# First decay rows of an attention and two-FFN kernel copied inside SBUF, its masks and loads issued in another order, and its first weight chunks loaded in pieces

## The chip, the cores and the metric

One core of a Trainium2 chip runs the whole program. The metric is the device time in microseconds (us) from launch to end; the median of the runs is quoted. The kernel is written with one program per engine: TensorE (PE, with its weight loads PEld), VectorE (DVE), ScalarE (ACT), GpSimd (POOL), and SyncE (SP), which here only issues DMA transfers.

## What is computed

The reference is a causal attention with a forgetting gate, and behind it two feed-forward layers:

```python
def _attn_ref(q, k, v, f):                 # (4, 8, 576, 64), f (4, 8, 576)
    scores = scale * np.matmul(q, k.transpose(0, 1, 3, 2))
    cum = np.cumsum(np.log(np.clip(f, 0.0001, 1.0)), axis=-1)
    decay = cum[:, :, :, None] - cum[:, :, None, :]
    scores = np.where(causal, -1000000000.0, scores + decay)
    attn = np.exp(scores - np.max(scores, axis=-1, keepdims=True))
    attn = attn / (np.sum(attn, axis=-1, keepdims=True) + 1e-09)
    return np.matmul(attn, v)
...
x = attn_out.transpose(0, 2, 1, 3).reshape(2304, 512)
h = x @ w_in;  x = (h - np.tanh(h)) @ w_out          # 512 -> 2048 -> 512
h = x @ w_in2; x = (h / (1 + np.exp(-h))) @ w_out2   # 512 -> 2048 -> 512
```

## The kernel before

**Attention.** The 32 heads are worked on as 16 pairs of heads. A pair has nine score tiles: four blocks of 128 query rows for each head, and one tile for the last 64 rows of both heads. A loop over `n` takes one tile in a step (line 734), 144 steps for 16 pairs and some to drain: PE makes the scores of tile n + 2, DVE takes the masked minimum of tile n (`least`, L497), ACT the exponential of tile n - 1 (L515), GpSimd divides three finished tiles by their row sums (`normalise`, L529), PE transposes tile n - 9 (L543), and two steps on it multiplies by the values (L588). All is in float32; each operand is split into a high and a low float32r part.

**Preparing a pair.** `load_kq` (L373) brings keys and queries of a pair (608 KB) into `kqraw`. `split` rounds them to `kqhi` (the keys on GpSimd, L393, the queries on DVE, L396) and makes `kqlo` as the rest on GpSimd (L384). `place` then copies both inside SBUF into the operand tiles `kqa` and `kqb` by DMA (L381): `place(p, 0)` six copies of `kqhi`, 608 KB for a head, 1216 KB in all; `place(p, 1)` four copies of `kqlo`, 608 KB; `place(p, 2)` reads four decay rows for each head from `dec` (L423). `kqraw` has two buffers, `kqhi` and `kqlo` one, the operand tiles two. Steps for pair p + 1 are hung on the loop by the table `prep`: the split from step 9p - 5 on, the places at 9p - 2 and 9p - 1, the load of pair p + 2 at 9p - 8.

**The decay rows.** `decay_rows` (L104) turns f into the cumulative log (a scan, L114) and four rows for each head that add the decay to the scores as a matmul. They are stored to DRAM as `dec` (L636) and read back. Pair 0 does without the operand tiles: its scores are four matmuls of 64 rows each (L459), the last of which takes the decay rows that `first_dec` (L412) reads from `dec` into `kqa0`; the tile of the last 64 query rows (L475) takes them from `last_q[2]`, a part of `ptl`.

**Order.** The order is that of the code (a manual schedule): each engine runs its instructions as they are written. SP issues all DMAs one after another. A DMA uses one of eight landing semaphores in turn, and waits for the landing of the one eight before it.

**The weights.** 32 chunks, each 512 KB of `w_in` and 512 KB of `w_out`, are loaded by `wload` (L135, DMA in L141) as 64-bit numbers and decoded in 14 stages (`wstages`, `wdecode`). For the first five chunks the stages `rest` (L177) and `join` (L181) run on GpSimd. Chunks 0 and 1 are loaded at steps 5 and 9 and their 28 stages done at steps 11 to 132, two in nine steps; each later chunk is loaded when the one two before it is decoded. Layers 1 and 2 (L256, L315) follow the attention.

Of the kernel before, what the change touches and what calls it, by code (L numbers as in the profile page):

```python
# [19 lines left out]
SCALE = 0.125  # L20
# [19 lines left out]
def forgetting_attention_two_ffn(  # L40
# [25 lines left out]
    def setup_mask(const):  # L66
# [8 lines left out]
        return mask, eps  # L75

    def setup_later(const):
        mask4 = const.tile([P, S // 2], F32, name="mask4")
        nc.gpsimd.memset(mask4, 0.0)
        for j in range(2):  # L80
            m = mask4[64 * j:64 * j + 64, S // 2 - 64:]
            nc.gpsimd.affine_select(
                out=m, in_=m, pattern=[[-1, 64]], compare_op=ALU.is_ge,
                fill=MASKED, base=0, channel_multiplier=1,
            )
        ident = const.tile([P, P], F32, name="ident")
# [5 lines left out]
        return mask4, ident  # L92
# [4 lines left out]
    C0, C1 = slice(S, S + 512), slice(S + 512, S + 576)  # L97

    def decay_consts(rows):
        nc.gpsimd.memset(rows[:, 0::2, S:RAW], 1.0 / SCALE)  # L100
        nc.gpsimd.memset(rows[:, 1::2, KQ], 1.0 / SCALE)
        nc.gpsimd.memset(rows[:, :, C1], 0.0)

    def decay_rows(rows, scratch, ft, meanwhile):  # L104
# [30 lines left out]
    def wload(k):  # L135
# [53 lines left out]
    def wdecode(k, left=0):  # L189
# [138 lines left out]
    def attention():  # L328
        with ExitStack() as actx:
# [56 lines left out]
            def split(p, j):  # L386
# [5 lines left out]
                if j == 0 and p:  # L392
# [226 lines left out]
            rows = room[:, 0:4 * RAW].rearrange("p (r w) -> p r w", w=RAW)  # L619
# [188 lines left out]
```

## Time and profile before

| what | value |
|---|---|
| median of 3 runs | 1026.9 us (1024.64 to 1027.33) |
| profiled execution, its own time | 1028.68 us |
| its span, first to last instruction | 1026.5 us |
| mean granted TensorE clock | 0.996 |
| PE busy | 990.1 us, 96% of the span |
| DVE, ACT, POOL busy | 59%, 48%, 19% |
| DMA moved | 83.71 MB |

The span is the profiled execution from its first to its last instruction; the device time has 2 us more around it. The page cuts the span into 40 slices of 25.7 us. Only in the first is PE busy less than eight tenths (3 of 10); from the second on it is at 7 and then 9. The DMA engines stand at 6 to 9 tenths in the first eight slices, which are the attention, and at 0 to 2 after it. A granted clock of 1.00 is 2.4 GHz, 0.50 is 1.2 GHz.

### The profile page before, as it was taken

What the parts mean: (1) busy time and instruction counts of PE and PEld (TensorE: products, weight loads), DVE (VectorE), ACT (ScalarE), POOL (GpSimd) and SP (SyncE); (2) the same over time, 40 slices, a digit from 0 to 9 for tenths busy, and PEclk for the clock granted to TensorE, in tenths of its full rate; (3) what the DMA queues carried; (4) which work ended last, traced back from release to release, by engine and by line L of the source; (5) the groups of instructions that cost most, each with busy time, mean ns of one, the idle gap of its engine ahead of it and who ended that gap; (6) DMA issues with size and microseconds to landing.
All of it is one profiled execution on the core that took longest, in us unless ns stands there. A gap on an engine that the chain in (4) does not pass through costs nothing.

```text
span 1026.5 us, 13933 instructions
## 1 busy us (share of the span) xinstructions
PE 990.1 (96%) x4928; PEld 828.3 (81%) x4928; DVE 608.5 (59%) x1382; ACT 492.5 (48%) x1092; POOL 200.2 (19%) x288
## 2 busy tenths in 40 slices
PE   3799999998999999999999999999999999999998
PEld 3577788777898888988888888888888888888887
DVE  4589888978686536666566774442552556633323
ACT  3588798885455333334343444343444344433222
POOL 5678987986000000000000000000000000000000
PEclk9999999999999999999999999999999999999999
DMA  6989999722211101110011220100110111001111
GB/s 158 289 233 236 265 234 243 198 94 84 82 59 66 42 1 42 61 64 29 14 41 42 83 82 0 42 28 35 62 30 12 42 42 42 1 1 42 41 42 62
DMA packets 28792, 83.71 MB, mean 82 GB/s; under 512 B 4340, under 2 KB 4340, under 8 KB 28692
## 3 DMA queue, kind: packets, MB, share of 16 engines
q1 hardware_dynamic: 28724, 82.83, 27.3%
q8 instruction: 39, 0.64, 0.3%
q14 instruction: 29, 0.24, 0.1%
HBM read 49.46 MB, written 5.34 MB: 53 GB/s over the span
## 4 chain that ended last, share of the span: by engine, by line
PE 88%; DVE 4%; DMA 4%; ACT 2%; SPq 2%; issue 1%; POOL 0%; DVEq 0%; ACTq 0%; POOLq 0%
PE a L315 38%; PE h L256 38%; PE out_t L588 4%; PE t L543 3%; SPq L381 1%; PE s L462 1%; PE s L463 1%; DMA kqb<-kqhi 1%; DMA kqa<-kqhi 1%; DVE kqhi L396 1%; PE s L479 1%; DVE ptl L570 1%; DMA kqraw<-kq 1%; PE misc L479 0%; ACT p L515 0%
## 5 line engine op out<-in xcount | busy, mean ns | idle before, releaser
L256 PE MATMUL h<-xh,wh 128*128 128x512 f32 (+1 forms) x640 | 237.2, 371 | 0.0
L256 PE MATMUL h<-xl,wh 128*128 128x512 f32 (+1 forms) x640 | 235.5, 368 | 0.0
L256 PE MATMUL h<-xh,wl 128*128 128x512 f32 (+1 forms) x640 | 235.5, 368 | 0.0
L278 DVE TENSOR_TENSOR gl<-g,gh 128x512 fp32r<-128x512 f32 (+1 forms) x158 | 101.4, 642 | 101.7 <-ACT gh L274 99.7
L274 ACT CAST gh<-g 128x512 fp32r<-128x512 f32 (+1 forms) x160 | 92.6, 579 | 95.9 <-DVE g L271 93.3
L256 PEld LDWEIGHTS h<-xh,wh 128*128 128x128 f32 x640 | 120.7, 189 | 21.1 <-issue 0.7
L256 PEld LDWEIGHTS h<-xl,wh 128*128 128x128 f32 x640 | 120.6, 188 | 21.0 <-issue 0.7
L256 PEld LDWEIGHTS h<-xh,wl 128*128 128x128 f32 x640 | 120.6, 188 | 20.1
L315 PE MATMUL a<-gh,wh 128*128 128x512 f32 (+1 forms) x320 | 117.9, 369 | 0.0
L315 PE MATMUL a<-gl,wh 128*128 128x512 f32 (+1 forms) x320 | 117.8, 368 | 0.0
L315 PE MATMUL a<-gh,wl 128*128 128x512 f32 (+1 forms) x320 | 117.7, 368 | 0.0
L315 PE MATMUL a<-wh,gh 128*128 128x512 f32 x288 | 112.2, 390 | 0.0
L315 PE MATMUL a<-wl,gh 128*128 128x512 f32 x288 | 112.2, 390 | 0.0
L315 PE MATMUL a<-wh,gl 128*128 128x512 f32 x288 | 112.0, 389 | 0.0
L273 ACT ACTIVATE g<-h 128x512 f32<-128x512 f32 (+1 forms) x80 | 44.3, 554 | 113.6 <-PE h L256 98.5
L244 DVE TENSOR_TENSOR xl<-y,xh 128x512 fp32r<-128x512 f32 (+1 forms) x60 | 37.4, 638 | 96.6 <-ACT xh L242 96.6
L242 ACT CAST xh<-y 128x512 fp32r<-128x512 f32 (+1 forms) x60 | 34.2, 579 | 104.8 <-PE h L256 103.1
L515 ACT ACTIVATE p<-p,mn 128x128 f32<-128x128 f32 (+3 forms) x128 | 72.2, 565 | 24.7 <-DVE mn L497 20.5
L529 POOL TENSOR_SCALAR p<-p,sm 128x128 f32<-128x128 f32 (+3 forms) x128 | 70.6, 565 | 19.4 <-DVE sm L526 14.8
L244 DVE TENSOR_TENSOR xl<-x,xh 128x512 fp32r<-128x512 f32 (+1 forms) x56 | 34.5, 634 | 62.3 <-ACT xh L242 62.3
L543 PE MATMUL t<-ident,p 128*128 128x128 f32 x320 | 59.6, 286 | 9.6 <-DVE sm L522 6.6
L315 PEld LDWEIGHTS a<-gh,wh 128*128 128x128 f32 x320 | 60.3, 189 | 10.4 <-ACT x L599 0.4
(136 smaller groups left out, 1705.2 us busy)
## 6 DMA issues: line engine op xcount, KB each, us to landing
raw<-w_in SPq DMA_DIRECT2D x32, 512.0 KB, 3.3
raw<-w_out SPq DMA_DIRECT2D x32, 512.0 KB
kqraw<-kq SPq DMA_DIRECT2D x16, 608.0 KB, 5.0
kqa<-kqhi SPq DMA_DIRECT2D x30, 304.0 KB, 4.7
vraw<-v SPq DMA_DIRECT2D x16, 320.0 KB, 5.3
kqa<-kqhi SPq DMA_DIRECT2D x30, 160.0 KB, 4.0
kqb<-kqlo SPq DMA_DIRECT2D x30, 160.0 KB, 3.1
out<-ob SPq DMA_DIRECT2D x18, 256.0 KB, 2.0
```

Source lines behind the costliest of these rows:

```text
L242: nc.scalar.copy(hi[:, :n], src[:, k, t0:t0 + n])
L244: eng.tensor_tensor(lo[:, :n], src[:, k, t0:t0 + n], rd(hi[:, :n]), ALU.subtract)
L256: nc.tensor.matmul(hp[:, :n], w[:, k * P:k * P + P], m[:, :n], start=(k == 0 and r == 0), stop=(k == NKT - 1 and r == 2),)
L273: nc.scalar.activation(g[:, :n], hp[:, :n], AF.Silu)
L274: nc.scalar.copy(gh[:, :n], g[:, :n])
L278: eng.tensor_tensor(gl[:, :n], g[:, :n], rd(gh[:, :n]), ALU.subtract)
L315: nc.tensor.matmul(dst, w, m, start=(first and r == 0), stop=(last and r == 2))
L381: nc.sync.dma_start(out=rd(out), in_=rd(in_))
L515: nc.scalar.activation(pt[:, :w], pt[:, :w], AF.Exp, bias=mn, scale=-1.0, accum_out=rowsum[n // 3][:, n % 3:n % 3 + 1],)
L529: nc.gpsimd.tensor_scalar(pt[:, :w], pt[:, :w], sm[:, j:j + 1], 1.0, ALU.mult, ALU.mult)
L543: nc.tensor.transpose(tp[:, c, :], pt[:, c * P:c * P + P], ident)
L588: nc.tensor.matmul(dst, w, pt[:, 448 * c + a:448 * c + q1], start=(c == 0 and r == 0), stop=(c == last and r == len(terms) - 1),)
```

## The change

- `first_dec` copies the decay rows of pair 0 from `rows` in SBUF to `kqa0`, one DMA for each of the four rows, two from SP's queue and two from ACT's. The tail parts for `last_q[2]` still come from `dec`, by `first_dec_last`, behind `place(1, 0)`.
- The rows in `rows` and `dec` are without the gap of 64 zeros (576 KB rather than 608 KB), so `place(p, 2)` is two DMAs, and the gap in `kqb` is set to zero once (GpSimd).
- Both masks, and the zeros of the operand tiles, are made on GpSimd ahead of the splits of pair 0; the identity stays late. Pair 1's first cast goes from GpSimd to DVE.
- `load_kq(2)` is issued ahead of `place(1, 1)`. The preparing of pair 2 comes two steps later, the loads of pair 3 four steps later.
- The loads of chunks 0 to 3 are cut into 4 pieces for each of the two matrices, 128 KB each. They go into a list, `trickle`, from which each step issues one. Chunk 0 starts at step 20, chunk 1 at step 36. The 28 stages lie on steps 40 to 132.

```diff
-        return mask, eps
-
-    def setup_later(const):
         mask4 = const.tile([P, S // 2], F32, name="mask4")
...
+        return mask, eps, mask4
+
+    def setup_ident(const):
...
-    C0, C1 = slice(S, S + 512), slice(S + 512, S + 576)
+    QS = slice(S, 2 * S)
...
-        nc.vector.tensor_copy(r(1, C0), cum[:, 0:512])
-        nc.vector.tensor_copy(r(1, TAIL), cum[:, 512:S])
-        nc.vector.tensor_tensor(r(3, C0), cum[:, 0:512], rows[:, 1, C0], ALU.subtract)
-        nc.vector.tensor_tensor(r(3, TAIL), cum[:, 512:S], rows[:, 1, TAIL], ALU.subtract)
+        split(0, 1)
+        nc.vector.tensor_copy(r(1, QS), cum)
+        nc.vector.tensor_tensor(r(3, QS), cum, rows[:, 1, QS], ALU.subtract)
...
-    def wload(k):
+    trickle = []
+
+    def wload(k, pieces=1):
...
+            to, n = r.rearrange("p n w -> p (n w)"), 2 * DM // pieces
+            for j in range(pieces):
+                trickle.append((to[:, n * j:n * j + n], (w_in, w_out)[m][l][c][:, n * j:n * j + n]))
             raws[k, m] = r
+        if pieces == 1:
+            begin(len(trickle))
+
+    def begin(n):
+        for to, source in trickle[:n]:
+            nc.sync.dma_start(out=to, in_=source)
+        del trickle[:n]
...
-                wload(k + 2)
+                wload(k + 2, 4 if k < 2 else 1)
...
-                if j == 0 and p:
+                if j == 0 and p > 1:
...
             def first_dec():
+                to = rd(first[2]).rearrange("(h r) w -> h r w", h=2)
+                for r in range(4):
+                    (nc.scalar if r % 2 else nc.sync).dma_start(
+                        out=to[:, r, 0:S + 512], in_=rows[0:2, r, 0:S + 512]
+                    )
+
+            def first_dec_last():
                 for h in range(2):
                     r = slice(64 * h, 64 * h + 4)
-                    nc.sync.dma_start(out=rd(first[2][r]), in_=dec[h])
-                    nc.sync.dma_start(out=rd(last_q[2][r, 64 * h:64 * h + 64]), in_=dec[h, :, TAIL])
+                    nc.sync.dma_start(out=rd(last_q[2][r, 64 * h:64 * h + 64]), in_=dec[h, :, S + 512:2 * S])
...
-                    nc.sync.dma_start(
-                        out=rd(tb[64:68, :, K0:W]), in_=dec[2 * p:2 * p + 2].rearrange("h r w -> r h w")
-                    )
+                    src = dec[2 * p:2 * p + 2].rearrange("h r w -> r h w")
+                    nc.sync.dma_start(out=rd(tb[64:68, :, K0:Z1]), in_=src[:, :, 0:S + 512])
+                    nc.sync.dma_start(out=rd(tb[64:68, :, Q1:W]), in_=src[:, :, S + 512:2 * S])
...
-            for h in range(2):
-                place(1, 0, [h])
-                place(1, 1, [h])
-                if h == 0:
-                    place(1, 2)
+            place(1, 0)
+            first_dec_last()
+            place(1, 2)
             load_kq(2)
+            place(1, 1)
             load_v(1)
...
-                                later(9 * p + k, fn, p + 1, j)
+                                later(9 * p + k + (2 if p == 1 else 0), fn, p + 1, j)
                         elif p + 2 < NP and (p or fn is load_v):
-                            later(9 * p + k, fn, p + 2)
+                            later(9 * p + k + (4 if p == 1 else 0), fn, p + 2)
...
-            ahead = {-N + 5: [(wload, 0)], -N + 9: [(wload, 1)], -12: [(open_earlier,)], 0: [(open_early,)]}
+            ahead = {-N + 20: [(wload, 0, 4)], -N + 36: [(wload, 1, 4)], -12: [(open_earlier,)], 0: [(open_early,)]}
...
-                at(9 * (k // 2 + 1) + (2, 6)[k % 2] - N, wdecode, k // NSTAGE, NSTAGE - 1 - k % NSTAGE)
+                at(40 + (N - 48) * k // (2 * NSTAGE) - N, wdecode, k // NSTAGE, NSTAGE - 1 - k % NSTAGE)
...
+                begin(1 if n < N else len(trickle))
```

How the instructions move. SP's queue at the start, before: after the store of `dec`, four reads of it for pair 0 and five copies for pair 1 come these rows (`kqraw2` is the load for pair 2, `raw0_0` weight chunk 0):

```order
L423 DMA kqb1_105<-dec_153 4x2x1216
L381 DMA kqa1_104<-kqhi1_163 64x1216
L381 DMA kqa1_104<-kqhi1_163 64x640
L381 DMA kqb1_105<-kqhi1_163 64x576
L381 DMA kqa1_104<-kqlo1_164 64x576
L381 DMA kqb1_105<-kqlo1_164 64x640
L373 DMA kqraw2_182<-kq 128x1216
L378 DMA vraw1_184<-v 128x640
L373 DMA kqraw3_232<-kq 128x1216
L141 DMA raw0_0_0_285<-w_in0 128x1024
L141 DMA raw0_0_1_287<-w_out0 128x1024
L423 DMA kqb0_103<-dec_153 4x2x1216
```

And now, from the decay rows of pair 0 (`kqa0<-x`) on:

```order
L424 DMA kqa0_102<-x_69 2x1088 x2
L657 DMA dec_168<-x_69 32x4608
L391 DMA kqa1_104<-kqhi1_170 64x1216
L391 DMA kqa1_104<-kqhi1_170 64x640
L391 DMA kqb1_105<-kqhi1_170 64x576
L391 DMA kqa1_104<-kqhi1_170 64x1216
L391 DMA kqa1_104<-kqhi1_170 64x640
L391 DMA kqb1_105<-kqhi1_170 64x576
L431 DMA ptl_111<-dec_168 4x64 x2
L440 DMA kqb1_105<-dec_168 4x2x1088
L441 DMA kqb1_105<-dec_168 4x2x64
L383 DMA kqraw2_188<-kq 128x1216
```

The load for pair 2 has moved ahead of the four copies of `kqlo1`, the two tail reads behind the six copies of `kqhi1`, and weight chunk 0 out of this stretch.

SP's queue where the pieces of chunk 0 now stand, between the load for pair 5 and the copies for pair 4:

```order
L383 DMA kqraw5_538<-kq 128x1216
L151 DMA raw0_0_0_563<-w_in0 128x256 x4
L151 DMA raw0_0_1_564<-w_out0 128x256
L440 DMA kqb0_103<-dec_168 4x2x1088
L441 DMA kqb0_103<-dec_168 4x2x64
L391 DMA kqa0_102<-kqhi4_602 64x1216
L391 DMA kqa0_102<-kqhi4_602 64x640
L391 DMA kqb0_103<-kqhi4_602 64x576
L391 DMA kqa0_102<-kqhi4_602 64x1216
L391 DMA kqa0_102<-kqhi4_602 64x640
L391 DMA kqb0_103<-kqhi4_602 64x576
L151 DMA raw0_0_1_564<-w_out0 128x256
```

Five pieces stand in a row ahead of `place(4, 2)` and `place(4, 0)`, one between `place(4, 0)` and `place(4, 1)`, and two behind it.

GpSimd's rows around the last stage of one matrix of chunk 0, before:

```order
L529 TENSOR_SCALAR p6_1_1_1416<-p6_1_1_1416,sm60_1436 128x256
L529 TENSOR_SCALAR p6_1_2_1441<-p6_1_2_1441,sm60_1436 128x384
L529 TENSOR_SCALAR p6_1_3_1471<-p6_1_3_1471,sm60_1436 128x512
L181 TENSOR_TENSOR wl0_0_0_764<-wl0_0_0_764,wb0_0_0_959 128x512
L393 TENSOR_SCALAR kqhi9_1573<-kqraw9_1320 128x576
```

The same stage now:

```order
L394 TENSOR_TENSOR kqlo10_1784<-kqraw10_1527,kqhi10_1783 128x320
L191 TENSOR_TENSOR wl0_0_0_1300<-wl0_0_0_1300,wb0_0_0_1435 128x512
L394 TENSOR_TENSOR vhl9_1913<-vraw9_1822,vhl9_1913 128x5x64
L545 TENSOR_SCALAR p8_1_1_1819<-p8_1_1_1819,sm78_1838 128x256
L545 TENSOR_SCALAR p8_1_2_1843<-p8_1_2_1843,sm78_1838 128x384
```

It has moved from a place directly ahead of a pair's `kqhi` to one behind its `kqlo`. Of the eight GpSimd stages of chunks 0 and 1, three stood directly ahead of a `kqhi` before and two do now.

## Rows read from the trace of the kernel before

**Rows 1.** Chain that ended last, in order of time: start us, us, what.

```profile
10.25 4.33 DMA dec<-x
...
24.49 5.13 DMA kqraw<-kq
...
128.61 3.05 DMA kqb<-kqlo
...
245.71 2.72 PE h L256 x12
```

**Rows 2.** By stretch: us; busy PE, PEld, DVE, ACT, POOL; clock; DMA share; GB/s.

```profile
14.60:27.58 12.98, 10.38 (x33) 8.38 (x33) 2.99 (x12) 3.49 (x10) 3.05 (x10) 1.00 0.77 169
...
45.25:59.59 14.34, 13.35 (x75) 10.83 (x74) 9.96 (x41) 9.83 (x31) 9.87 (x16) 0.88 0.94 251
59.59:71.29 11.70, 11.57 (x75) 9.56 (x74) 10.69 (x40) 10.40 (x33) 9.71 (x16) 1.00 0.90 238
...
107.13:120.51 13.38, 11.49 (x75) 9.54 (x74) 12.03 (x41) 10.46 (x34) 11.98 (x18) 1.00 0.91 250
120.51:133.85 13.34, 13.07 (x75) 10.91 (x74) 9.46 (x39) 10.14 (x30) 10.80 (x17) 0.87 0.97 265
```

**Rows 3.** Timeline of PE: start us, us, what, [idle before <- what ended it].

```profile
16.80 0.44 PE L459 MATMUL s<-kqa 64*128 64x128 f32 x1 [7.54 <-DMA kqa<-dec]
...
22.00 0.44 PE L475 MATMUL s<-kqa,ptl 128*128 128x288 f32 x1
...
31.13 0.79 PE L459 MATMUL s<-pth 64*128 64x512 f32 x1 [3.96 <-DVE mn L497]
...
33.14 0.47 PE L462 MATMUL s<-kqa 128*128 128x128 f32 x1
...
44.30 0.41 PE L543 MATMUL t<-ident,p 128*128 128x128 f32 x2 [3.20 <-DVE sm L522]
...
45.31 0.31 PE L462 MATMUL s<-kqa 128*128 128x128 f32 x1
```

**Rows 4.** Timeline of DVE at the start, same columns.

```profile
8.74 1.42 DVE L120 SCALAR_TENSOR_TENSOR x<-x 32x576 fp32r<-32x576 f32 x1
...
10.09 0.52 DVE L396 CAST kqhi<-kqraw 128x640 fp32r<-128x640 f32 x1
...
17.40 0.29 DVE L497 CUSTOM_DVE_ANT_0 p<-s,mask 128x128 f32<-128x128 f32 x1 [6.79 <-POOL mask L82]
...
29.84 0.49 DVE L396 CAST kqhi<-kqraw 128x640 fp32r<-128x640 f32 x1 [4.44 <-DMA kqraw<-kq]
...
43.06 0.49 DVE L396 CAST kqhi<-kqraw 128x640 fp32r<-128x640 f32 x1 [2.65 <-DMA kqb<-kqhi]
```

**Rows 5.** Timeline of SP's DMA queue: issue us, us of issuing, what.

```profile
15.98 1.16 SPq L381 DMA_DIRECT2D kqa<-kqhi  x2
...
26.49 0.43 SPq L141 DMA_DIRECT2D raw<-w_in  x1
...
30.89 2.81 SPq L381 DMA_DIRECT2D kqa<-kqhi  x2
...
56.22 0.58 SPq L373 DMA_DIRECT2D kqraw<-kq  x1
...
59.59 0.27 SPq L423 DMA_DIRECT2D kqb<-dec  x1
```

**Rows 6.** Weight loads by line (L141), from issue to landing.

```profile
DMA to landing us min/median/max: 3.2/3.3/4.0
```

**Rows 7.** Busy time in the two us from 46.00, columns as in rows 2.

```profile
46.00:48.00 2.00, 2.00 (x8) 1.62 (x8) 2.00 (x10) 0.91 (x4) 2.00 (x4) 0.50 1.04 394
```

**Rows 8.** DVE's casts of one line from 45 to 205 us: ns min/median/max.

```profile
L396 DVE CAST kqhi<-kqraw x12: 487/494/2833, 57.4 to 191.2; 128x640 fp32r<-128x640 f32 x12
```

**Rows 9.** Timeline around the longest of these casts, DVE and GpSimd.

```profile
115.98 2.83 DVE L396 CAST kqhi<-kqraw 128x640 fp32r<-128x640 f32 x1
...
116.56 1.27 POOL L181 TENSOR_TENSOR wl<-wl,wb 128x512 fp32r<-128x512 f32 x1
```

More of the change, by code (lines that the diff above doesn't have):

```diff
@@ L64, in rd, with setup_masks @@
         return ap.bitcast(F32)
-    def setup_mask(const):
+    def setup_masks(const):
         mask = const.tile([P, 640], F32, name="mask")
@@ L91, in setup_later, with decay_rows @@
         )
-        return mask4, ident
+        return ident
     BH = B * H
-    C0, C1 = slice(S, S + 512), slice(S + 512, S + 576)
+    QS = slice(S, 2 * S)
     def decay_consts(rows):
-        nc.gpsimd.memset(rows[:, 0::2, S:RAW], 1.0 / SCALE)
+        nc.gpsimd.memset(rows[:, 0::2, QS], 1.0 / SCALE)
         nc.gpsimd.memset(rows[:, 1::2, KQ], 1.0 / SCALE)
-        nc.gpsimd.memset(rows[:, :, C1], 0.0)
-    def decay_rows(rows, scratch, ft, meanwhile):
+    def decay_rows(rows, scratch, ft, split):
         ones, lf, cum = scratch
@@ L111, in decay_rows @@
         nc.scalar.activation(lf, ft, AF.Ln)
-        for fn, *a in meanwhile:
-            fn(*a)
         nc.vector.tensor_tensor_scan(cum, ones, lf, 0.0, ALU.mult, ALU.add)
+        split(0, 0)
         nc.scalar.mul(r(0, KQ), cum, -1.0)
-        nc.vector.tensor_copy(r(1, C0), cum[:, 0:512])
-        nc.vector.tensor_copy(r(1, TAIL), cum[:, 512:S])
-        nc.vector.tensor_tensor(r(3, C0), cum[:, 0:512], rows[:, 1, C0], ALU.subtract)
-        nc.vector.tensor_tensor(r(3, TAIL), cum[:, 512:S], rows[:, 1, TAIL], ALU.subtract)
+        split(0, 1)
+        nc.vector.tensor_copy(r(1, QS), cum)
+        nc.vector.tensor_tensor(r(3, QS), cum, rows[:, 1, QS], ALU.subtract)
         nc.vector.scalar_tensor_tensor(r(2, KQ), cum, -1.0, rows[:, 0, KQ], ALU.mult, ALU.subtract)
@@ L140, in wload @@
             r = rawp.tile([P, DM, 2], U32, tag="raw", name=f"raw{l}_{c}_{m}")
-            nc.sync.dma_start(out=r.rearrange("p n w -> p (n w)"), in_=(w_in, w_out)[m][l][c])
+            to, n = r.rearrange("p n w -> p (n w)"), 2 * DM // pieces
+            for j in range(pieces):
+                trickle.append((to[:, n * j:n * j + n], (w_in, w_out)[m][l][c][:, n * j:n * j + n]))
             raws[k, m] = r
+        if pieces == 1:
[4 more added lines that the diff above has]
+        del trickle[:n]
     def wstages(k):
@@ L618, in attention @@
             room = x.rearrange("p k t -> p (k t)")[0:BH]
-            rows = room[:, 0:4 * RAW].rearrange("p (r w) -> p r w", w=RAW)
-            ft, *scratch = (room[:, 4 * RAW + S * j:4 * RAW + S * j + S] for j in range(4))
+            rows = room[:, 0:8 * S].rearrange("p (r w) -> p r w", w=2 * S)
+            ft, *scratch = (room[:, S * j:S * j + S] for j in range(8, 12))
             nc.sync.dma_start(out=ft, in_=f)
@@ L625, in attention @@
             nc.vector.memset(scratch[0], 1.0)
-            nc.vector.memset(rd(first[2]), 0.0)
+            nc.vector.memset(rd(first[2][:, 0:S + 512]), 0.0)
+            decay_consts(rows)
+            mask, eps, mask4 = setup_masks(const)
+            for ta, tb in kqt[::-1]:
+                nc.gpsimd.memset(rd(ta[:, :, 0:K0]), 0.0)
+                nc.gpsimd.memset(rd(tb[:, :, 0:K0]), 0.0)
+                nc.gpsimd.memset(rd(tb[64:68, :, Z1:Q1]), 0.0)
+            decay_rows(rows, scratch, ft, split)
+            first_dec()
             nc.vector.memset(rd(ptl[:, RAW:RAW + 384]), 0.0)
-            decay_consts(rows)
-            decay_rows(rows, scratch, ft, [(split, 0, 0), (split, 0, 1)])
-            mask, eps = setup_mask(const)
             split_last(0)
@@ L634, in attention @@
             split_last(1)
-            dec = dram.tile([BH, 4, RAW], F32, name="dec")
+            dec = dram.tile([BH, 4, 2 * S], F32, name="dec")
             nc.sync.dma_start(out=dec, in_=rows)
-            first_dec()
-            for t in kqt[1] + kqt[0]:
-                nc.gpsimd.memset(rd(t[:, :, 0:K0]), 0.0)
             for j in range(6):
                 split(1, j)
-            for h in range(2):
-                place(1, 0, [h])
-                place(1, 1, [h])
-                if h == 0:
-                    place(1, 2)
+            place(1, 0)
+            first_dec_last()
+            place(1, 2)
             load_kq(2)
+            place(1, 1)
             load_v(1)
@@ L651, in attention @@
                 nc.gpsimd.memset(a[:, S:640], 0.0)
-            mask4, ident = setup_later(const)
+            ident = setup_ident(const)
             scores(tiles[0])
```

## The prediction

> **What bounds the kernel now.** I read the chain of waits first, then the time by stretch, then the timelines of PE, DVE and SP's queue at the start. From 245.71 us on the chain is PE alone, twelve matmuls in 2.72 us, one group behind another [rows 1]: nothing that the change touches can shorten the layers, except by letting them begin earlier. So the question is when the attention ends.
>
> The stretches between two issues of decay rows are one pair long. An undisturbed pair takes 11.70 us with PE busy for 11.57 of them [rows 2]: in the steady state PE is the limit, and the DMA engines, at 0.90, are close behind. The start is different. PE waits 7.54 us for the first decay rows [rows 3], which go to DRAM for 4.33 us [rows 1] and back. It waits 3.96 us before 31.13 [rows 3]: it needs a score buffer that DVE has not emptied, since DVE stood 4.44 us at the cast of pair 2's queries [rows 4], whose load was issued only at 24.49 and took 5.13 us [rows 1]. It waits 3.20 us before 44.30 [rows 3]: DVE stood at the cast for pair 3, because the copies of pair 2 had not yet read `kqhi` [rows 4]; they were issued at 30.89, behind weight chunk 0 at 26.49 [rows 5]. After that wait the granted clock is 0.50 around 46 to 48 us [rows 7], that is 1.2 GHz, and the stretch from 45.25 takes 14.34 us [rows 2].
>
> **The change part by part.** The sum is made against the profiled execution, 1028.68 us.
>
> *First decay rows.* DVE ends them at 8.74 + 1.42 = 10.16 [rows 4]; merging two pairs of instructions can only make this earlier. Before, `dec` had landed at 10.25 + 4.33 = 14.58 [rows 1] and the rows read back released PE at 16.80 [rows 3], 2.2 us for issue and landing. With the same 2.2 us from 10.2 the first scores are ready by 12.4, 4.4 us earlier. The masks, for which DVE last waited at 17.40 [rows 4], are made by GpSimd before that. But the gain doesn't stay whole: the tail tile needs `last_q[2]`, still read from `dec`, behind the six copies of `place(1, 0)`. These start at about 10.9 (DVE's casts at 10.09, 0.52 us each [rows 4], one more now), are issued in 6 × 0.58 = 3.5 us [rows 5], and move 1216 KB, at 238 GB/s [rows 2] 5.2 us. The tail rows land at 10.9 + 5.2 = 16.1 if the store of `dec` costs these copies nothing, and at 14.6 + 5.2 = 19.8 if it goes wholly first. PE's own work would bring it there at 12.4 + (22.00 − 16.80) = 17.6 [rows 3]. I take 19.1, near the upper end, because DMA at the start moves only 169 GB/s [rows 2]. Gain: 22.00 − 19.1 = **2.9 us** (0 to 4.4).
>
> *Load of pair 2.* It is now behind the six copies, two tail reads and two reads of `dec`, no longer behind ten copies: issue near 17 rather than 24.49, landing by 22.2 with the same 5.13 us [rows 1]. DVE gets to that cast when PE gets to its neighbour in the loop, at 31.13 − 2.9 − 3.96 = 24.3 [rows 3], and it now comes one tile later. The wait of 3.96 us goes: **3.96 us** (3 to 4). Next is `place(1, 1)`, late because of the load now ahead of it, but it lands near 24, and pair 1's scores come at 33.14 − 2.9 − 3.96 = 26.3 [rows 3].
>
> *Wait for pair 2's copies.* From pair 1's first scores to pair 2's were 45.31 − 33.14 = 12.2 us, 3.20 of them the wait [rows 3]. Without chunk 0 in front, and with the split two steps later, `place(2, ·)` runs from about 25: 1824 KB and the decay rows at 238 GB/s [rows 2] take 7.8 us, and with the loads of 3 us around them they land near 36. PE would want them at 26.3 + 9.0 = 35.3. I take 2.6 of the 3.20 us as gained: **2.6 us** (0.5 to 3.2).
>
> *Clock after the wait.* The stretch of 14.34 us exceeds its neighbour by 2.6 [rows 2]. With no wait of three us ahead of it, most goes: **2.3 us** (1 to 2.6).
>
> *Weights in pieces.* 2 MB that went in beside the start's waits are now moved while PE is the limit: 16 pieces for 4 loads, and 16 more for 4 in chunks 2 and 3; 24 more issues with 15 second decay reads are 39 more on SP. The two decay rows issued on ACT fall before its first exponential. A step issues one piece, but in SP's queue nothing holds a piece back, as its buffer is free: five run as soon as the load for pair 5 is out. SP was empty there from 56.22 + 0.58 to 59.59 [rows 5] but for one load, so part is hidden. The nearest row for an unhidden chunk is the stretch from 120.51, behind the load of chunk 2, where the last copy of a pair, at 128.61, is in the chain [rows 1]: 13.34 against 11.70 [rows 2], 1.6 us. Chunks 0 and 1 cost between 0 and 3.3 us together; I take **−2.4 us**, nearer the upper end, because the last pieces stand between the copies. Chunk 2 moves to another pair at the same price; chunk 3 comes when no copies are left.
>
> The Trainium skill, "DMA: Bandwidth & Descriptors", section "Bandwidth", speaks against pieces: it wants transfers of 1 MiB or more, with about 2.0 us fixed in each, which as an estimate is 18 us for eight pieces one after another. The trace has loads of 512 KB landing in 3.2 to 4.0 us with several in flight [rows 6], and none of 128 KB; I see the fixed part as overlapped.
>
> *Decode stages.* 28 stages lie on 92 rather than 121 steps. On GpSimd the price is not their length but where they stand: of twelve casts on DVE the median is 494 ns and one took 2833 [rows 8], at 115.98, while GpSimd ran `join` for 1.27 us [rows 9]; that stretch took 13.38 us [rows 2]. Three stages stood directly ahead of a `kqhi` and one did this; now two do. I count **0** (−1.7 to +1.7).
>
> The Trainium skill, "SBUF — State Buffer", section "Who interferes with whom", says that a cast in a two-port mode and a GpSimd instruction exclude each other for a whole instruction, and that the order of issue decides; the 2.83 us beside 0.49 agree, and by it the sign here hangs on drift that no row tells.
>
> *At nothing:* the masks, zeros and the cast moved to DVE, covered by the wait for `last_q[2]`; without that cover DVE's cast costs 0.5 us [rows 4].
>
> **Sum:** 2.9 + 3.96 + 2.6 + 2.3 − 2.4 = 9.4 us. The profiled execution would go to 1019.3; the median stands 1.8 us under it, so I forecast 1026.9 − 9.4 = **1017.5 us**.
>
> **Rivals.**
> - *The direct copy does nothing in the end:* the tail rows through DRAM land as late as PE came there before, and the first term is 0: 1020.4 us. For it: 19.8 is the upper end only if the queue adds no more. Against: PE then still finds loads and masks done.
> - *Pieces at full price:* each chunk disturbs two pairs as between 107.13 and 133.85, 13.38 + 13.34 − 2 × 11.70 = 3.3 us, 6.6 for two chunks: 1021.7 us. For it: DMA at 0.90 and up. Against: half of those 3.3 us came from the cast.
> - *No blocked cast and free pieces:* neither `join` nor pieces cost anything and the 1.7 us at 115.98 go: 1026.9 − 11.8 − 1.7 = 1013.4 us.
> - *Slower, by pieces ahead of the copies:* the pieces hold a pair's copies past the end of the pair before, PE stands, and the clock falls as at 46 us. A pair hit like that costs 2.6 us [rows 2]. Chunks 0 to 2 touch six pairs, 15.6 us against 11.8 gained: 1030.7 us. It decides from the fifth pair on. Against it: chunk 2 whole, in front of one pair, cost 1.6.
>
> **How the numbers follow.** A measurement of this kernel tells about 0.3%, 3.1 us, from no change: faster is under 1023.8, slower over 1030.0. Forecast 0.50; first rival 0.16; pieces at full price 0.15; none blocked 0.10; slower 0.04; and 0.05 that the start's gains are taken back by pair 2's copies, near 1025. Faster: 0.50 + 0.16 + 0.10 + most of 0.15, 0.89; within 0.3% 0.07; slower 0.04. The range is 1012.5 to 1023.0: the third rival with the first term at its bound of 4.4 gives 1013.4 − 1.5 = 1011.9, pieces at full price with the third term at its bound of 0.5 give 1021.7 + 2.1 = 1023.8, and I cut 0.6 and 0.8 from these, as both ends need two bounds at once.
>
> **What would show it.** Right: PE's first decay matmul near 12, the tail tile near 19, pair 1's scores near 26, pair 2's near 36, no cast waiting for a load, no clock of 0.50 near 46 us, and pairs 3 to 6 at about 12.3 us each. Wrong: PE waiting for `kqb` or `kqa` copies in pairs 3 to 6, several casts over 2 us, or a clock of 0.50 behind such waits.

## The result, and the profile after

The change made the kernel slower: 1035.9 us median of 5 runs (1033.02 to 1037.51) against 1027.33 us of the kernel before on the same chip (1024.64 to 1030.08); the ratio is 1.0079, 95% interval 1.0052 to 1.0107. The forecast was 1017.5 us, with 0.04 for slower. The profiled execution took 1036.97 us, its span is 1035.1 us against 1026.5.

The page of the changed kernel: its head, PE and DMA in 40 slices of 25.9 us, the chain that ended last by engine.

```profile
span 1035.1 us, 13990 instructions
...
PE   5769999998999999999999999999999999999998
...
DMA  7969999833121101120111210101100111001111
...
PE 82%; DMA 5%; DVE 4%; SPq 4%; POOL 2%; ACT 2%; issue 2%; DVEq 0%; POOLq 0%; ACTq 0%
```

PE is now at 5 in the first slice (3 before), but at 7 and 6 in the next two, where before had 7 and 9. So the start went faster, and something right behind it is slow. PE's timeline tells where (start us, us, what, idle time before and what ended it):

```profile
18.94 0.61 PE L491 MATMUL s<-kqa,ptl 128*128 128x288 f32 x1 [2.26 <-DMA ptl<-dec]
...
25.92 0.47 PE L478 MATMUL s<-kqa 128*128 128x128 f32 x1
...
38.07 0.66 PE L559 MATMUL t<-ident,p 128*128 128x128 f32 x2 [5.08 <-DVE sm L538]
...
39.87 0.46 PE L478 MATMUL s<-kqa 128*128 128x128 f32 x1
...
68.75 0.61 PE L495 MATMUL misc<-kqa 128*128 128x288 f32 x1 [7.96 <-ACT x L615]
```

The tail tile begins at 18.94 (22.00 before) and the scores of pair 1 at 25.92 (33.14) [rows 3]: 7.2 us won. Then a wait of 5.08 us stands where before had 3.20, and the scores of pair 2 begin at 39.87, 5.4 us ahead of 45.31 [rows 3]. Then PE stands for 7.96 us before 68.75, where before had no wait of 3 us or more. The stretches tell the same (columns as in rows 2, one pair each):

```profile
39.61:52.95 13.34, 13.21 (x75) 11.20 (x74) 8.78 (x36) 8.83 (x28) 9.23 (x16) 0.85 0.81 215
52.95:75.16 22.21, 14.25 (x75) 11.61 (x74) 9.93 (x39) 10.13 (x32) 11.41 (x18) 0.77 0.62 169
75.16:86.70 11.54, 11.40 (x76) 9.58 (x75) 9.81 (x39) 10.40 (x32) 7.43 (x13) 1.00 0.90 225
```

One pair takes 22.21 us; the same stretch of before, 59.59 to 71.29, took 11.70 [rows 2]. PE says it waited for ACT, but ACT itself was waiting. First ACT's timeline, then SP's DMA queue (issue us, us of issuing, what):

```profile
67.23 0.46 ACT L456 CAST vhl<-vraw 128x320 fp32r<-128x320 f32 x1 [8.84 <-DMA vraw<-v]
```

```profile
53.97 1.38 SPq L391 DMA_DIRECT2D kqa<-kqhi  x2
...
61.63 0.59 SPq L391 DMA_DIRECT2D kqb<-kqlo  x1
62.26 1.06 SPq L151 DMA_DIRECT2D raw<-w_out  x2
63.42 0.40 SPq L388 DMA_DIRECT2D vraw<-v  x1
63.86 0.43 SPq L383 DMA_DIRECT2D kqraw<-kq  x1
74.51 0.33 SPq L388 DMA_DIRECT2D vraw<-v  x1
```

ACT stood 8.84 us at the cast of pair 3's values (`prep_v(3)`, L456), to which it came at 67.23 − 8.84 = 58.39. SP issued their load only at 63.42, behind the ten copies for pair 4, which it issued from 53.97 to 62.2 with one piece of chunk 0 among them and two behind. The load landed 3.8 us later. Behind that cast in ACT's order stood the copy `x` (L615), for which PE waited; GpSimd stood 9.32 us and DVE 8.97. With all of them idle the granted clock is 0.50 for 10.2 us from 64.1 on. In windows of two us it reads, columns as in rows 7:

```profile
64.00:66.00 2.00, 0.00 (x0) 0.00 (x0) 0.00 (x0) 0.00 (x0) 0.00 (x0) 0.52 1.02 269
70.00:72.00 2.00, 2.00 (x9) 1.71 (x8) 1.85 (x8) 1.98 (x6) 0.96 (x2) 0.50 0.00 0
```

In the first no compute engine works at all; in the second PE works without a pause at 1.2 GHz, and the DMA engines are empty, because SP's next issue waits for PE until 74.51.

**Where the load went.** The table `prep` hung `load_v(3)` on step 24 and `prep_v(3)` on step 28. I read the edit `+ (4 if p == 1 else 0)` as one on the keys' load; it moves `load_v(3)` too, to step 28, the step of the cast that reads it. On step 24 the load stood ahead of the copies for pair 4, which hang on steps 25 and 26; on step 28 it stands behind them in SP's queue.

### The profile page after: what moved, and what is told of

It is laid out like the page before. It is cut to its first block, busy times and chain, and to the rows that moved or that the text cites. A ratio compares the mean times of both kernels' runs of the same rounds, so it can differ in the third digit from the quotient of the medians.

```text
span 1035.1 us, 13990 instructions
## 1 busy us (share of the span) xinstructions
PE 992.8 (96%) x4928; PEld 830.3 (80%) x4928; DVE 604.8 (58%) x1381; ACT 492.7 (48%) x1092; POOL 200.7 (19%) x288
## 4 chain that ended last, share of the span: by engine, by line
PE 82%; DMA 5%; DVE 4%; SPq 4%; POOL 2%; ACT 2%; issue 2%; DVEq 0%; POOLq 0%; ACTq 0%
PE a L325 38%; PE h L266 38%; SPq L391 3%; PE out_t L604 2%; DMA kqb<-kqhi 2%; PE t L559 1%; DMA vraw<-v 1%; POOL p L545 1%; PE s L478 1%; PE s L479 1%; ACT p L531 1%; DMA kqb<-kqlo 1%; DMA kqraw<-kq 1%; POOL kqlo L394 1%; DVE ptl L586 1%
```

## The experiments

Times are medians beside runs of the kernel before on the same chip; ratios are to these, with 95% intervals. The first scores of a pair and the first `h` matmul of the layers are read from PE's timeline of each run, in us:

| kernel | pair 1 | 2 | 3 | 4 | 15 | first `h` | span |
|---|---|---|---|---|---|---|---|
| before | 33.1 | 45.3 | 59.6 | 71.3 | 205.6 | 220.4 | 1026.5 |
| the change | 25.9 | 39.9 | 53.0 | 75.2 | 214.0 | 228.9 | 1035.1 |
| change, values early (`e1`) | 25.9 | 38.3 | 50.9 | 62.9 | 207.2 | 222.0 | 1028.2 |
| `e1`, weights as before (`e6`) | 26.0 | 44.2 | 59.2 | 71.5 | 207.4 | 222.2 | 1028.4 |
| before, weights as in the change (`e7`) | 31.7 | 41.5 | 53.2 | 68.3 | 210.3 | 226.3 | 1032.3 |
| before, dense stages (`e10`) | 33.6 | 45.2 | 61.6 | 73.0 | 207.2 | 224.8 | 1030.8 |

### Is it the load of pair 3's values?

`e1_v3_early`, the change with that load left in its old step:

```diff
-                            later(9 * p + k + (4 if p == 1 else 0), fn, p + 2)
+                            later(9 * p + k + (4 if p == 1 and fn is load_kq else 0), fn, p + 2)
```

> The changed kernel with the values of pair 3 loaded at step 24 again instead of step 28, where ACT's cast of the same values stands; everything else as changed. Theory V (the moved load meets its reader in the same step, and ACT, then DVE and PE, wait 8 us): the wait of 8.84 us of ACT for vraw goes, no granted clock of 0.50 near 70 us, and the time falls by 9 to 11 us from 1035.9, to about 1025.5, level with or a little under the kernel before. Rival P (the pieces of the weights stand in SP's queue and everything behind them is late, wherever the values' load is written): the load stays late, 1032 or more.

Measured: 1028.27 us (1026.53 to 1031.84), ratio 1.0007 (0.9993 to 1.0021): 7.6 us under the change, where 9 to 11 were expected. Stretches of `e1`, columns as above:

```profile
50.90:62.90 12.00, 11.48 (x75) 9.53 (x74) 9.77 (x41) 10.28 (x34) 9.86 (x16) 1.00 0.90 237
62.90:76.90 14.00, 11.68 (x76) 9.60 (x74) 9.82 (x40) 10.68 (x33) 9.87 (x16) 1.00 1.02 263
```

The stretch of 22.21 us takes 12.00. The load is issued at 50.02 there, ahead of the copies for pair 4, and its cast runs at 56.16 without a wait.

`e4_before_v3_late`, the other way round: the kernel before with this load alone four steps later.

```diff
-                            later(9 * p + k, fn, p + 2)
+                            later(9 * p + k + (4 if p == 1 and fn is load_v else 0), fn, p + 2)
```

> The kernel before with one edit: the values of pair 3 loaded at step 28 instead of 24. Theory V: ACT waits for them there too, 4 to 8 us of it, and the clock falls behind the wait: 1033 to 1037. Rival P: there are no pieces in the queue here, so no change, 1027.

Measured: 1035.95 us, ratio 1.0082 (1.006 to 1.0103). PE's waits of this kernel between 40 and 76 us (what waited <- for what: us in total, times, longest):

```profile
PE misc L479 <- ACT x L599: 5.0, 1, 5.0
...
```

It is the same wait, in the other kernel, and the same 8 us; there too SP issues the load, at 65.83, behind the ten copies for pair 4. Taken out of the change it gives back 7.6 us; put alone into before it costs 8. This cause is settled.

### Is it the pieces of the weights?

`e2_whole_chunks` (the change) and `e3_v3_early_whole` (on `e1`) load the chunks whole in the same steps:

```diff
-                wload(k + 2, 4 if k < 2 else 1)
+                wload(k + 2)
...
-            ahead = {-N + 20: [(wload, 0, 4)], -N + 36: [(wload, 1, 4)], ...
+            ahead = {-N + 20: [(wload, 0)], -N + 36: [(wload, 1)], ...
```

> The changed kernel with every weight chunk loaded in two whole transfers again (chunk 0 still begun at step 20, chunk 1 at step 36), the values of pair 3 still at step 28. Theory V: ACT still waits for the values, since they are asked for in the step that reads them; 1033 to 1037. Rival P: without the pieces in front the load lands in time, 1025 to 1027.

> Both: values of pair 3 at step 24 and whole chunks. Theory V: like the run with the early values alone, within 2 us, about 1025.5; what differs between the two is the price of the pieces by themselves. Rival P: about 1025 too, but then the run with the early values alone must be at 1032 or more.

Measured: `e2` 1037.55 us, 1.0085 (1.0059 to 1.0111), against the change's 1.0079; `e3` 1027.39 us, 0.9998 (0.9981 to 1.0016), against `e1`'s 1.0007. The intervals overlap in both couples. In `e2` PE waits 5.7 us at the same place as in the change. The pieces make no difference that these runs can tell.

### Is it the second read of the decay rows?

`e5_one_decay` gives `e1` the old row layout and one read for each pair; `e8_before_two_decay` gives before two reads (the gap in `kqb`, which it sets to zero once, is not in these lines):

```diff
-                    nc.sync.dma_start(
-                        out=rd(tb[64:68, :, K0:W]), in_=dec[2 * p:2 * p + 2].rearrange("h r w -> r h w")
-                    )
+                    src = dec[2 * p:2 * p + 2].rearrange("h r w -> r h w")
+                    nc.sync.dma_start(out=rd(tb[64:68, :, K0:Z1]), in_=src[:, :, 0:S + 512])
+                    nc.sync.dma_start(out=rd(tb[64:68, :, Q1:W]), in_=src[:, :, TAIL])
...
```

> The run with the early values, with the old layout of the decay rows (gap of 64 zeros in rows and dec), so that each pair's decay rows are read in one DMA again; the first rows still go from SBUF to SBUF. Theory D (the second decay read of each pair stands ahead of the copies of kqhi in SP's queue and in the turn of the eight semaphores; kqhi has one buffer, so the next cast, then DVE and PE, come later by some 0.4 us in each of 11 to 13 pairs): 4 to 6 us less than 1028.3, 1022 to 1024. Rival W (what takes the start's gain back is the time of the weights: their pieces, and 28 decode stages on 92 steps): no change, 1027 to 1029.

> The kernel before with each pair's decay rows read by two DMAs, as in the change (the gap of zeros set once), and nothing else. Theory D: 0.4 us in each of 11 to 13 pairs, 1031 to 1033. Rival W: no change, 1027 to 1028.

Measured: 1027.44 us, 0.9997 (0.9978 to 1.0016), and 1027.32 us, 0.9997 (0.9983 to 1.0011). Neither matters.

### Where does the start's gain go?

With the values early, pair 4 begins 8.4 us ahead of before (62.9 against 71.3), and pair 15 begins 1.6 us behind (207.2 against 205.6). Eleven pairs take 144.3 us in place of 134.3. `e6_weights_back` (on `e1`) and `e7_before_weights_late` (on before) exchange the place of the weights, with whole chunks in both; the diff is that of `e6`, `e7` goes the other way:

```diff
...
-            ahead = {-N + 20: [(wload, 0, 4)], -N + 36: [(wload, 1, 4)], ...
+            ahead = {-N + 5: [(wload, 0)], -N + 9: [(wload, 1)], ...
...
-                at(40 + (N - 48) * k // (2 * NSTAGE) - N, wdecode, ...
+                at(9 * (k // 2 + 1) + (2, 6)[k % 2] - N, wdecode, ...
```

> The run with the early values, with the weights as before: chunks 0 and 1 whole at steps 5 and 9, the stages at steps 11 to 132. Theory D: the two decay reads stay, so the pairs stay long; the weights are again in the start, where they cost: 1027 to 1031. Rival W: the pairs are as short as before, 11.6 to 12.2 us, and the start's gain is kept but for the weights' own time in it: 1020 to 1024.

> The kernel before with only the weights' times of the change (whole chunks, begun at steps 20 and 36, stages on steps 40 to 132). Theory D: the start gets shorter by the weights' loads there, 3 to 5 us, and the pairs stay as before, so 1022 to 1025. Rival W: the gain of the start is taken back by longer pairs, 1026 to 1030.

Measured: `e6` 1027.16 us, 0.9988 (0.9971 to 1.0005); `e7` 1029.55 us, 1.0016 (0.9995 to 1.0036). In `e6` PE's timeline has a wait that takes the start's gain at once:

```profile
41.50 0.66 PE L559 MATMUL t<-ident,p 128*128 128x128 f32 x2 [7.57 <-DVE sm L538]
```

The clock is 0.50 for 10.2 us from 38.7 on, and pair 4 begins at 71.5, as in before. So the earlier start needs the weights out of its way; that part of the change does what it seems to do.

What it costs later stands in the table too. With the weights back, the eleven pairs take 135.9 us in `e6` against 144.3 in `e1`, and PE's waits in them are 4.8 us in all against 12.9. What the weights' new place wins up to pair 4, 8.6 us, it loses behind it, and the times are hardly apart (1.0007 and 0.9988). The size is that of single executions: `e3`, like `e1` but with whole chunks as in `e6`, takes 137.8. But the kernels of this document fall into groups, and the first two do not overlap:

| eleven pairs from 4 to 15 | kernels | us | mean | PE's waits in them |
|---|---|---|---|---|
| loads and stages of chunks 0 and 1 as in before | before, `e4`, `e6`, `e8`, `e11`, `e15`, `e17` | 132.7 to 135.9 | 134.2 | 3.5 to 4.8 |
| both moved | the change, `e1`, `e2`, `e3`, `e5`, `e7`, `e12`, `e14`, `e16`, `e18` | 137.8 to 144.3 | 140.7 | 5.9 to 12.9 |
| stages alone moved | `e10`, `e13` | 134.2, 137.0 | | 4.4, 5.4 |
| both moved, chunks 1 to 3 not loaded | `e9` | 136.3 | | 7.8 |

So the weights' new place costs some 6.5 us of the lead in these pairs. Theory W was nearly right on the pairs and wrong on the start.

`e10_before_dense` is before with the second edit of `e7` alone (the stages on steps 40 to 132).

> The kernel before with only the decode stages of chunks 0 and 1 moved to steps 40 to 132, the loads of these chunks at steps 5 and 9 as before. Theory C: the bytes are where they were, so no change but for single blocked casts, 1025 to 1029. Rival W: the denser stages lengthen the pairs from 40 on by 0.5 us or more each, 1031 to 1035.

Measured: 1030.59 us, 1.0046 (1.003 to 1.0062). The stages, moved alone, cost 4.7 us by the ratio and 3.7 by the medians. But not in the eleven pairs, which take 134.2 us, as in before; `e7`, which moves the loads as well, takes 142.0 there (its profiled execution is its slowest, 1034.53 us). This speaks for the loads as what makes the pairs longer; no run moves them alone. The span of `e10` is 4.3 us longer than before's: 1.6 us stand at pair 15's first scores, and 2.8 more are gone by the first `h`. There its timeline shows DVE, GpSimd and PE:

```profile
208.62 2.94 DVE L522 TENSOR_TENSOR sm<-sm,eps 128x3 f32<-128x3 f32 x1
...
209.04 1.28 POOL L181 TENSOR_TENSOR wl<-wl,wb 128x512 fp32r<-128x512 f32 x1
...
210.28 1.26 POOL L244 TENSOR_TENSOR xl<-x,xh 128x512 fp32r<-128x512 f32 x1
...
212.22 0.44 PE L462 MATMUL s<-kqa 128*128 128x384 f32 x1 [1.92 <-DVE mn L497]
```

DVE's `guard`, three columns, is recorded with 2.94 us; its median in this trace is 0.17. It ends at 211.56, 0.02 us after the second of two GpSimd instructions in a row. PE waits 1.92 us and then has a clock of 0.50 for 3.4 us. This is no single case: in nine kernels, all with the stages moved, a `guard` near this place takes 2.94 to 2.99 us, and the first `h` comes 16.0 to 17.6 us behind pair 15; in the other eleven it comes 14.8 or 14.9 us behind. The profiles of the change and of `e1` are among the eleven.

**The guard.** The Trainium skill, "SBUF — State Buffer", section "Who interferes with whom", says that a VectorE instruction with two inputs in SBUF contends with a GpSimd instruction that reads SBUF, and one with a single input does not, outside the two-port modes. `guard` has two such inputs. Three kernels give it one (`e13` is `e10` with this edit, `e14` is `e1`, `e15` is before):

```diff
-                nc.vector.tensor_tensor(sm, sm, eps, ALU.add)
+                nc.vector.tensor_scalar(sm, sm, 1e-9, None, ALU.add)
```

> The kernel before with the decode stages of the first two weight chunks moved as the change moves them (the version that took 1030.6 us, 4.7 over before), and the guard (the sum of the row sums and 1e-9, 128x3) made an operation with a constant and one SBUF input in place of two. Theory G (what the dense stages cost is the guard held up on VectorE beside two GpSimd stages back to back: 2.94 us for an operation whose median is 0.17, and the low clock after it): the guard's longest is under 1 us, the gap of 1.92 us in PE near 212 us and the low clock after it are gone, and the time is 1027 to 1028.5 us. Theory Q (GpSimd's own queue is the cost: normalise and kqlo wait for the stages whatever VectorE does): the guard is short, and the time stays at 1030 to 1031.

> The change with pair 3's values loaded in their old step (the version that took 1028.3 us, 1.0007 of before), and the guard with a constant and one SBUF input. Theory G: the waits of PE for the guard between 72 and 205 us (9.2 us in 8 of them) fall under 3 us, the gap near 205 us is gone, and the time is 1022 to 1025 us. Theory Q: PE waits as long for another operation, and the time is 1027 to 1029.

> The kernel before with the guard alone changed to one SBUF input. It is the control of the two runs beside it: theory G has 6.6 us of PE waits for the guard in six places to win, so 1023 to 1026 us; theory Q has no change, 1026.5 to 1028.

Measured: `e13` 1031.64 us, 1.0033 (1.002 to 1.0046); `e14` 1028.08 us, 1.0002 (0.9986 to 1.0017); `e15` 1028.15 us, 1.0006 (0.9993 to 1.0018). In `e14` PE's waits for the guard between 72 and 205 us are 6.6 us, where theory G asked for under 3. The timeline of `e13` at the same place:

```profile
207.41 2.97 DVE L522 TENSOR_SCALAR sm<-sm 128x3 f32<-128x3 f32 x1
...
209.09 1.26 POOL L244 TENSOR_TENSOR xl<-x,xh 128x512 fp32r<-128x512 f32 x1
...
211.04 0.45 PE L462 MATMUL s<-kqa 128*128 128x384 f32 x1 [1.95 <-DVE mn L497]
```

With one input it is held as long, and again it ends with the second GpSimd instruction (210.38 and 210.35). So theory G fell in the form in which it was put, and the number of inputs does not explain the hold; whether this form runs in a two-port mode the trace does not tell.

`e16_v3_early_stages_vector` takes `rest` and `join` of chunks 0 and 1 off GpSimd:

```diff
-        eng = nc.gpsimd if k < NEARLY + MID else nc.vector
+        eng = nc.gpsimd if 2 <= k < NEARLY + MID else nc.vector
```

> The change with pair 3's values loaded in their old step, and the last two stages of the first two chunks' decode (rest and join, four of 128x512 a chunk) on VectorE in place of GpSimd. Theory G: with no GpSimd stage of 1.27 us back to back with another, no guard is held up, and the time is 1023 to 1026 us, less what the eight operations cost on VectorE (about 0.6 us each, beside its idle time). Theory Q: GpSimd's queue is shorter by eight stages of 1.27 us, and the time falls as far; so this run speaks for both where the two with the guard alone tell them apart. If it stays at 1028, neither holds.

Measured: 1028.19 us, 1.0003 (0.9986 to 1.0021). Pair 4 begins at 63.5 and pair 15 at 203.4, 139.9 us for the eleven pairs against 144.3; the median is `e1`'s, and `e5` (139.9) and `e14` (140.3) are as quick there with the stages on GpSimd. The times of `e13` and `e14` are those of theory Q, but with GpSimd's queue eight stages shorter the time should then fall; so neither theory holds.

**The bytes.** `e9_v3_early_no_load` decodes chunks 1 to 3 from chunk 0's bytes and does not load them:

```diff
...
+        if 0 < k < 4:
+            for m in range(2):
+                raws[k, m] = raws[0, m]
+            return
...
```

> The run with the early values, without the loads of chunks 1 to 3: these are decoded from the raw numbers of chunk 0, so the output is not that of the reference, and 1 MB less goes through the DMA queue in pairs 4 to 6, 1 MB less in pairs 9 to 11, 1 MB less behind the last copies; every decode stage stays. Theory C (the copies for the pairs keep the DMA engines and the chain of kqhi, copies and casts busy, so each chunk loaded before the last pair costs its own 3 to 4 us wherever it stands; that is why the shorter start is given back): the pairs with chunks 1 and 2 go from 13 or 14 us to about 12, 5 to 8 us less than 1028.3, so 1020 to 1023. Rival W (the 28 decode stages on 92 steps make the pairs long): no change, 1027 to 1029.

`e11_before_chunk2_held` (on before) and `e12_v3_early_chunk2_held` (on `e1`) load chunk 2 at step 126, behind most of the pairs:

```diff
-            if not stages[k]:
+            if not stages[k] and k:
...
+            at(126 - N, wload, 2)
```

> The kernel before with one edit: chunk 2 is loaded at step 126, behind the last copies for a pair, where the DMA engines stand at 0.3, instead of at step 69 amid them; its decoding begins at step 145. Theory C: the pair behind step 69 goes from 13.3 to about 12 us, 1 to 3.5 us less, 1024 to 1026. Rival W: no change, 1027.

> The run with the early values, and chunk 2 loaded whole at step 126 instead of in pieces at steps 85 to 92. Theory C: 2 to 4 us less than 1028.3, 1024 to 1026. Rival W: no change, 1028.

Measured: `e9` 1025.51 us, 0.9981 (0.9969 to 0.9994), 2.8 us under `e1` where 5 to 8 were expected; `e11` 1026.44 us, 0.9994 (0.9983 to 1.0004); `e12` 1028.68 us, 1.0014 (1.0001 to 1.0026). In its profile `e9` comes near the first group; but its pair 4 begins at 65.4, and it has the long `guard`, so less of this reaches the time. By the times, weight bytes are a part of it at most, and the place of chunk 2 makes no difference that these runs can tell.

**The copies.** The casts into the one `kqhi` buffer must wait until the copies of the pair before have read it. Groups of instructions between 72 and 205 us, first of before, then of `e1`: busy us, mean ns | idle just before, and what ended it.

```profile
L396 DVE CAST kqhi<-kqraw 128x640 fp32r<-128x640 f32 x10 | 8.9, 891 | 0.9 <-DMA kqa<-kqhi 0.9
L393 POOL TENSOR_SCALAR kqhi<-kqraw 128x576 fp32r<-128x576 f32 x10 | 7.8, 784 | 3.9 <-DMA kqb<-kqhi 3.0 <-DMA kqa<-kqhi 1.0
```

```profile
L403 POOL TENSOR_SCALAR kqhi<-kqraw 128x576 fp32r<-128x576 f32 x10 | 8.5, 854 | 12.0 <-DMA kqa<-kqlo 5.4 <-DMA kqb<-kqhi 3.9 <-DMA raw<-w_out 2.4
...
L406 DVE CAST kqhi<-kqraw 128x640 fp32r<-128x640 f32 x10 | 7.2, 718 | 7.9 <-DMA kqa<-kqlo 3.1 <-DMA kqb<-kqhi 2.4 <-DMA raw<-w_out 1.9
```

Before 0.9 and 3.9 us of waiting, in `e1` 7.9 and 12.0, at a DMA share of 0.90 in both. Of these 19.9 us in `e1`, 14.8 are put down to copies of the pair before and 4.3 to a weight load. In `e6`, with the weights back, the same casts wait 2.8 and 6.4 us. Over the first two groups of the table above, the two casts together wait 3.0 to 9.2 and 8.6 to 19.9 us. The last two kernels take the values' loads of pairs 4 to 15 (some 320 of 2790 KB a pair) off the queue, in before and in `e1`:

```diff
+                if p > 3:
+                    vraw[p] = vraw[p - 3]
+                    return
```

> The kernel before, with the values of pairs 4 to 15 not loaded: they are read from the tiles of pairs 1 to 4, so the output is not the reference's. It takes 320 KB of some 2790 KB that a pair moves over the DMA engines, which are 0.90 busy between 72 and 205 us at 236 GB/s; 1.4 us of their time a pair. It is the control of the run beside it. Theory B (the DMA engines' occupancy sets the pace of pairs 4 to 15, through the copies that free the one kqhi buffer): before has 3.9 us of waits of the POOL cast and 0.9 of the DVE cast for the copies to win, so 1023 to 1027 us. Theory N (the pace is set by the compute engines among each other): no change, 1026.5 to 1028.

> The change with pair 3's values loaded in their old step (1028.3 us, 1.0007 of before), and the values of pairs 4 to 15 not loaded, as in the run beside it; the output is not the reference's. Theory B: with a ninth of a pair's bytes gone the casts' waits for copies (12.0 us on POOL and 7.9 on DVE between 72 and 205 us, against 3.9 and 0.9 in before) fall by more than half, the pairs take 12.2 us or less, most of the 8 us lead at pair 4 is kept, and the time is 1018 to 1022 us, 3 us or more under the run beside it. Theory N: the pairs still take 13 us, the lead is given back, and the time is 1026 to 1029, that of the run beside it.

Measured: 1026.01 us, 0.9977 (0.9966 to 0.9989), and 1026.46 us, 0.9989 (0.9971 to 1.0008). The casts of `e18`, same view and stretch:

```profile
L406 POOL TENSOR_SCALAR kqhi<-kqraw 128x576 fp32r<-128x576 f32 x10 | 8.0, 798 | 5.4 <-DMA kqa<-kqlo 2.4 <-DMA kqa<-kqhi 1.4 <-POOL p L548 1.1
L409 DVE CAST kqhi<-kqraw 128x640 fp32r<-128x640 f32 x10 | 6.6, 663 | 3.8 <-DMA kqa<-kqlo 1.9 <-DMA kqa<-kqhi 0.9 <-POOL p L548 0.6
```

The casts' waits fell by more than half, as theory B had it, and the pairs still do not run at 12.2 us: pair 4 begins at 63.8 and pair 15 at 203.6, 139.8 us for eleven. The time is that of the run beside it. Theory B fails by its own number.

**What stays open.** That the pairs are longer with the weights in their new place, and that most of the lead goes there, the groups of kernels show; the long `guard` takes 1.2 to 2.8 us more where it occurs. That the loads do it more than the stages is indicated by `e7` beside `e10` and by the profile of `e9`, and not shown. In what way they do it is not settled. Each of the suspects taken alone (pieces, second decay reads, GpSimd's stages, the guard's second input, weight bytes, a ninth of the pairs' bytes) gave 0 to 2.8 us. None of the versions is faster than before by 0.3%. Two suspects taken out together, and a second `kqhi` buffer, were not tried.

## Why the prediction was wrong, step by step

**First decay rows: right.** The tail tile was put at 19.1 and began at 18.94, a gain of 3.06 where 2.9 was forecast, and what PE waited for there, 2.26 us, was the tail rows through `dec`, as forecast.

**Load of pair 2: right.** Pair 1's scores were put at 26.3 and began at 25.92. DVE's casts in the changed kernel show this step and the next:

```profile
24.35 0.49 DVE L406 CAST kqhi<-kqraw 128x640 fp32r<-128x640 f32 x1 [0.88 <-DMA kqa<-kqlo]
...
36.83 0.49 DVE L406 CAST kqhi<-kqraw 128x640 fp32r<-128x640 f32 x1 [4.53 <-DMA kqb<-kqlo]
```

At 24.35, where before waited 4.44 us for the load [rows 4], it waits 0.88, and for a copy.

**Wait for pair 2's copies: wrong, nothing was gained.** I had the copies land near 36, which is right: the cast was released at 36.83. The step that failed is "PE would want them at 35.3". It asked when PE needs pair 2's operands. The first to need these copies gone is DVE: the cast for pair 3, which overwrites the buffer they read, stands in DVE's order ahead of `guard`, and DVE came to it at 36.83 − 4.53 = 32.3. The copies landed 6.2 us earlier than before (36.83 against 43.06), but DVE came to the cast 8.1 us earlier (32.3 against 43.06 − 2.65 = 40.41 [rows 4]), so the wait grew from 3.20 to 5.08 us; the term is −1.8, not +2.6 (7.2 us ahead at pair 1, 5.4 at pair 2). The sign is that of one execution. Eight profiles whose code is the same up to there (the change, `e1`, `e2`, `e3`, `e9`, `e12`, `e16`, `e18`) have waits from 1.54 to 5.08 us, 3.1 on average; four of before's start (before, `e4`, `e11`, `e17`) have 3.00 to 3.78, 3.3 on average. So on average the wait got shorter by some 0.1 us, where 2.6 were forecast.

**Clock after the wait: wrong, with it.** The wait stayed, and the low clock with it. Of the changed kernel:

```profile
38.00:40.00 2.00, 1.93 (x8) 1.67 (x8) 2.00 (x12) 1.10 (x4) 1.39 (x3) 0.50 0.80 261
```

The stretch after it takes 13.34 us against 14.34 [rows 2]: 1.0 of the 2.3 us.

**The loads of pair 3: the largest miss, and no term at all.** My account of the change took every DMA that is moved at the start to its queue, but "four steps later" I followed for the keys alone, and the values' reader, `prep_v(3)`, stands four steps behind the old place of the load; the ten copies between the old and the new place were not counted either. It cost 10.2 us in its own stretch (22.21 against 12.00 in `e1`) and 8 at the end.

**Weights in pieces: too low, and not by the pieces.** I charged 2.4 us for 2 MB moved into the pairs. The pieces themselves show no cost: by the ratios they are 0.9 us dearer than whole chunks in `e1` and 0.6 cheaper in the change, with overlapping intervals. But loads and stages in their new place cost some 6.5 us in pairs 4 to 15 (the mean of 140.7 against 134.2). This comes near the rival that ends slower, by which the weights hold a pair's copies back and PE stands: the casts wait longer in that group, and PE with them (5.9 to 12.9 us against 3.5 to 4.8). Its low clock hardly came (once in these pairs of the change, 3.4 us), and that the time landed past its 1030.7 is luck: 8 us of it are the values of pair 3.

**Decode stages: counted 0, bounds ±1.7.** In before, moved alone, they cost 3.7 us by the medians and 4.7 by the ratio (interval 1.003 to 1.0062, some 3 to 6 us). I had counted how many stand ahead of a `kqhi`, and not which stand next to another GpSimd instruction beside a `guard`. In the change's own profile this price is not to be seen: its longest `guard` takes 1.87 us, and the first `h` comes 14.9 us behind pair 15.

**The sum.** The profile of the change is 8.6 us longer than that of before, where 9.4 less were forecast: 18.0 us apart. The first two terms came out 0.4 better (7.2 us at pair 1 where 6.9 were forecast). The third and fourth are 5.7 worse (2.6 + 1.8 and 2.3 − 1.0). Pair 3's stretch is 10.5 us longer than before's (22.21 against 11.70), nearly all of it the values' load. Pairs 4 to 15 take 138.8 us against 134.3, of which 2.4 were charged: 2.1 more. Together that is 17.9. I expected the lead to stand, less what the pieces take: a gain at the start was taken as one at the end, since 11.70 us a pair looked like PE's own limit [rows 2].

## What to carry to other kernels

When a table of steps is shifted, list every function that the shift reaches, and for each load the step of its first reader: one that is issued in its reader's step, behind copies that are queued already, stops the engine that reads it and all that stands behind the reader in its order. Ask who overwrites a buffer as well as who reads it: here the next cast, not the next matmul, was the one in need of the copies. And a lead at the start is worth its length at the end only if the pairs behind it run no slower. Loads that are taken out of the start go somewhere, and here most of what that won was lost again behind it; read the times at several points, as in the table above, before a gain is counted.

## What was not expected of the hardware

A VectorE instruction of 128x3 was recorded with 2.94 us beside two GpSimd instructions of 1.28 and 1.26 us in a row, where its median in that trace is 0.17, and with one SBUF input in place of two it took 2.97. It ended 0.02 and 0.03 us after the second of them. The long cast of before [rows 9] had two beside it as well: behind the `join` of that row GpSimd's cast of the keys ran from 117.80 to 118.46, and DVE's cast ended at 118.81.

And the low clock reached past the wait. In the change it fell while PE still stood, at 36.8 and at 64.1 us, and stayed at 0.50 for 6.8 and 10.2 us. PE's waits of 5.08 and 7.96 us ended at 38.07 and 68.75, so in both places PE worked on at half speed for 5.5 us.
